# Late attention scores as plain float32 on quarters of the array, three rooms for loads and one store a pair

## The chip, the cores and the metric

The kernel runs on one core of one Trainium2 chip. The metric is the time of one execution on the device, in microseconds (us); less is better. All inputs and the output are float32 in HBM.

## What is computed

Banded attention with a linear bias for 4 batches, 8 heads, 768 positions and 64 numbers a head, and behind it a two-layer perceptron on the 3072 tokens.

```python
scores = (1 / sqrt(D)) * q @ k.T
is_global = pos[None, :] < n_global            # 8
is_local = (rel >= 0) & (rel < n_local)        # 96
dist = where(is_global & ~is_local, n_local, abs(rel))
scores = where(is_global | is_local, scores - slopes[h] * dist, -1e9)
a = exp(scores - max(scores))
x = (a / (sum(a) + 1e-9)) @ v                  # 3072 x 512
h = x @ w_in                                   # 512 x 2048
out = (h * clip(h + 3, 0, 6) / 6) @ w_out      # 2048 x 512
```

## The kernel before

The tokens are cut into 8 blocks of 384 (`TB`), each in three tiles of 128 queries (`NT`). A block has four pairs of heads, so there are 32 pairs, `n` = 0 to 31. A query tile sees 232 keys (`W`): 96 ahead of the tile, 8 global ones, and its own 128. Pairs 0 to 8 (`EARLY`) are early, 9 to 31 late.

The layers. Float32 matrices are split into a high and a low part of type float32r, and a product is three matmuls (high with high, low with high, high with low). For one of 16 slices `f` of the middle dimension, `first` (L168) does 12 matmuls of 384 columns into `hp`; `gate` (ScalarE L179, VectorE L180) makes `g`; `high` makes `gh` (L186 on GpSimd or L188 on ScalarE) and `rest` makes `gl` (L193, VectorE); `second` (L200) does 9 matmuls of 512 columns into `acc`. `twos` takes two slices at a time: both `first` parts, two places for other work ("units"), both `second` parts of the two slices before, two units more. So 32 units make up a block's layers, and the attention of the next block is put into them by `attention`; `rest_of_third` does the same in the stage before, with one slice at a time (a half slice is one unit).

The attention of a pair. `load` brings keys, queries and values into a room (`load0` and so on) in SBUF; keys and queries come first, values when the room's values are used up. Early pairs take their scores as plain float32 on half the rows of TensorE for each head (`scores`, L857). Late pairs split queries and keys first (`split`: L831 ScalarE, L832 GpSimd, L835 and L838 VectorE), both parts one above the other in the rows, and take two float32r matmuls for each head and tile (L861): 12 a pair, 232 columns each (128 for the first tile of a batch). `weigh` adds distances and takes the minimum on VectorE (L872), then the exponential with its sum on ScalarE (L876). `sum_up` (L886, L887, VectorE) inverts the sums, `normalize` (L896, GpSimd) multiplies. Then keys must come into the rows. Early pairs are turned on TensorE (`turn`, L904 and L906, copied out at L908 as `pt`). Late pairs are turned by VectorE in squares of 32 (`spread`, L921), stored to `there` in DRAM (L923, one store a tile), and fetched back in another order (`fetch`, L930, four a pair) as `weights`. `values` (L948) multiplies with v: plain float32, each head on one half of the array's columns, 12 matmuls a pair (10 for the first block of a batch). `put_x` (L154, L155) puts the result into `xh` and `xl`.

In the layers stage, a block's late pairs are six units apart; the values of two pairs stand together behind the second one, six units after its fetch. One bank `sp`, one bank `tp` and one bank `xp` are for attention; a tile's scores for both heads go to one bank, and tiles take `sp` and `tp` in turn.

The early stage is followed by a stage in which the weight matrices are decoded from 64-bit words (`decode`, L410 to L427, mostly VectorE), with layer steps of blocks 0 and 1 in an order written by hand (`ORDER`). Instructions of TensorE, GpSimd and SP keep the order in which the code writes them (`in_order`); those of VectorE and ScalarE are placed by a scheduler.

Of the kernel before, what the change touches and what calls it, by code (L numbers as in the profile page):

```python
# [33 lines left out]
QW = 2 * TB  # L34
# [3 lines left out]
SLOPES = [2.0 ** (-8.0 * (h + 1) / H) for h in range(H)]  # L38
LEAST, MOST = (float(np.uint32(e << 20).view(np.float32)) for e in (896, 1151))
# [4 lines left out]
ROOMS = 2  # L44
# [15 lines left out]
class Kernel:  # L60
# [162 lines left out]
    def attending(self, ctx, heads, rows, ps, **kw):  # L223

        if heads:
            self.hp = self.pool("hp", heads, ctx=ctx, **kw)
# [53 lines left out]

    def rooms(self, pool, n, start=0):

        return [pool.tile([P, LOAD], F32, name=f"load{start + i}") for i in range(n)]
# [4 lines left out]
    def load(self, n, values):  # L288

        if n < len(self.blocks) * NPAIR:  # L290
            end = KW + (TB if n < EARLY else QW)
# [12 lines left out]
    def loaded(self, n):  # L304
# [3 lines left out]
        q = at[:, KW:KW + QW].rearrange("p (j t c) -> p j t c", j=2, t=NT)  # L308
# [30 lines left out]
    def banded_setup(self):  # L339
# [7 lines left out]
        for n in range(ROOMS):  # L347
# [164 lines left out]
    def banded(self, flag):  # L512
# [12 lines left out]
        with ExitStack() as early, ExitStack() as words:  # L525
# [10 lines left out]
            with ExitStack() as ctx:  # L536
                self.room += self.rooms(self.pool("more", 1, ctx=ctx), MORE - ROOMS, ROOMS)
                self.load(2, False)
                self.fetch(1)
                for n in range(ROOMS):  # L540
                    self.load(n, True)
                self.plain_distances(ctx)
                self.attending(ctx, 0, 9, 5)
# [52 lines left out]
            self.weights()  # L596
            self.allowed = 4 * (2 * NF + 1)
# [9 lines left out]
        self.attending(self.ctx, 2, 3, 2, side="right")  # L607
        self.bp = self.pool("bp", 3, side="right")
        self.there = self.pool("there", 2, bass.MemoryType.DRAM)
# [39 lines left out]
    def rest_of_third(self, x, slices):  # L649
# [3 lines left out]
        for k in range(3):  # L653
            pairs[0].split(k, False)
        units[1] += [lambda: self.load_next(EARLY, False)]
        for p, (me, after) in enumerate(zip(pairs, pairs[1:])):
            at = units[4 * p + 1:]
            last = after is pairs[-1]
            at[0] += [lambda t=t, me=me: me.scores(t)() for t in range(NT)]
            at[1] += [me.sum_up] + [lambda t=t, me=me: me.normalize(t) for t in range(NT)]  # L660
            at[2] += [lambda t=t, me=me: me.spread(t) for t in range(NT)] + [me.fetch]
            for k in range(3):
                at[k + 3 if last else k].append(lambda k=k, after=after: after.split(k))
# [4 lines left out]
    def attention(self, i, x, first):  # L668
# [4 lines left out]
        for p in range(NPAIR):  # L673
# [11 lines left out]
            for t in range(1, NT if after else 0):  # L685
                at[t + 3].append(lambda t=t, after=after: after.split(t))
# [115 lines left out]
class Pair:  # L802
# [4 lines left out]
    def __init__(self, kernel, n, x, plain):  # L807
# [4 lines left out]
        self.parts = [{}, {}]  # L812

    def low(self, t):
        return CB if self.tb == 0 and t == 0 else 0

    def split(self, step, load=True):
# [3 lines left out]
        k, q, _, _ = kk.loaded(self.n)  # L821
        c = slice(CB if self.tb == 0 else 0, None)
        for j, part in enumerate(self.parts):
            h = 2 * self.pr + j
            scale = float(-1.0 / (np.sqrt(D) * SLOPES[h]))
            own, other = (slice(0, D), slice(D, P)) if j == 0 else (slice(D, P), slice(0, D))
            if step == 0:
                part["q1"] = kk.hp.tile([P, NT, P], F32R, name="q1")
                part["q2"] = kk.hp.tile([P, NT, P], F32R, name="q2")
                part["kx"] = kk.hp.tile([P, KW], F32R, name="kx")  # L830
                nc.scalar.mul(out=part["q1"], in_=q[:, j], mul=scale)  # L831
                nc.gpsimd.tensor_scalar(out=part["kx"][own, c], in0=k[own, c], scalar1=1.0, scalar2=0.0,  # L832
                                        op0=ALU.mult, op1=ALU.add)
            elif step == 1:
                nc.vector.scalar_tensor_tensor(out=part["q2"], in0=q[:, j], scalar=scale, in1=part["q1"].bitcast(F32),  # L835
                                               op0=ALU.mult, op1=ALU.subtract)
            else:
                nc.vector.tensor_tensor(out=part["kx"][other, c], in0=k[own, c], in1=part["kx"][own, c].bitcast(F32),  # L838
                                        op=ALU.subtract)
        if step == 2 and load:  # L840
            kk.load_next(self.n, False)

    def scores(self, t):
# [3 lines left out]
        if t != 1 or not self.plain:  # L847
            self.banks = [kk.bank("s")[:, 0:2 * W].rearrange("p (i c) -> p i c", i=2) for _ in range(2 if self.plain else 1)]
        sp = [self.banks[j][:, t % 2] if self.plain else self.banks[0][:, j] for j in range(2)]
# [4 lines left out]
        for j in range(2):  # L854
            if self.plain:
                rows = slice(j * D, (j + 1) * D)
                nc.tensor.matmul(sp[j][:, lo:W], lhsT=queries[rows, 0, t], rhs=keys[rows, c], start=True, stop=True)  # L857
            else:
                part = self.parts[j]
                for m, q in enumerate((part["q1"], part["q2"])):  # L860
                    nc.tensor.matmul(sp[j][:, lo:W], lhsT=q[:, t], rhs=part["kx"][:, c], start=(m == 0), stop=(m == 1))  # L861
        return lambda: self.weigh(t, sp, e, lo)

    def weigh(self, t, sp, e, lo):
        nc, kk = self.nc, self.k
        for j in range(2):
# [3 lines left out]
            else:  # L870
                d, scale = (kk.d0 if lo else kk.d1), SLOPES[h]
            nc.vector.tensor_tensor_reduce(out=e[:, j, lo:W], in0=sp[j][:, lo:W], in1=d, op0=ALU.add, op1=ALU.min, scale=scale,  # L872
                                           scalar=3.0e38, accum_out=self.least[:, i:i + 1])
        for j in range(2):
            i = 2 * t + j
            nc.scalar.activation(out=e[:, j, lo:W], in_=e[:, j, lo:W], func=AF.Exp, bias=self.least[:, i:i + 1], scale=-1.0,  # L876
# [12 lines left out]
    def normalize(self, t):  # L889
        nc, e, lo = self.nc, self.rows[t], self.low(t)  # L890
        for j in range(2):
            over = self.sums[:, 1, 2 * t + j:2 * t + j + 1]
            if self.n == 0:
                nc.vector.tensor_scalar(out=e[:, j, lo:W], in0=e[:, j, lo:W], scalar1=over, scalar2=None, op0=ALU.mult)
            else:
                nc.gpsimd.tensor_scalar(out=e[:, j, lo:W], in0=e[:, j, lo:W], scalar1=over, scalar2=0.0, op0=ALU.mult, op1=ALU.add)  # L896
# [14 lines left out]
    def spread(self, t):  # L911
# [3 lines left out]
        if t == 0:  # L915
            self.weights = kk.tp.tile([P, 4, NT, 2, 2, 32], F32, name="weights")
            self.there = kk.there.tile([P, 4, NT, 2, 2 * 32], F32, name="there")
        blocks = kk.bp.tile([P, 4, 2, 2, 32], F32, name="blocks")
        parts = slice(1 if self.low(t) else 0, None)
        for s, c in ((0, 0), (1, CB))[parts]:  # L920
# [107 lines left out]
```

## Time and profile before

| | us |
|---|---|
| median of 3 runs (660.98 to 661.49) | 661.33 |
| the profiled execution | 660.32 |
| its span, first to last instruction | 658.5 |
| TensorE busy (98%) | 647.1 |
| VectorE busy (64%) | 423.2 |
| ScalarE busy (43%) | 286.4 |
| GpSimd busy (29%) | 189.1 |

The stages in that execution: the early pairs to about 59 us, decoding with layers to 151 us, the first three late pairs to 199 us, and layers with the attention of the next block to the end. The granted TensorE clock is 1.000.

How to read the lines below: PE is TensorE, DVE VectorE, ACT ScalarE, POOL GpSimd, SPq the queue of DMA issues on SyncE. L861 is line 861 of the kernel. A piece of the chain gives its start and length in us, engine, tile and line, and how many instructions it merges. A group or a timeline row gives its output and inputs, the part of the array for TensorE (rows by columns), the shape, and, behind the bar, busy us and mean ns, then idle time ahead and what ended it. A matmul's own duration in a row runs to its modelled end; what counts on TensorE is the distance from one start to the next. "xN, KB, us" in the DMA table is the median from issue to landing.

### The profile page before, as it was taken

The page shows a single profiled execution, that of the slowest core. Times are in us where ns is not written, and L with a number is a line of the kernel's source. Part 1 is how long each engine was busy: PE and PEld are TensorE (multiplying, and loading weights), DVE is VectorE, ACT ScalarE, POOL GpSimd, SP SyncE. Part 2 cuts the span into 40 slices and gives each one's busy share as a digit, 9 for nine tenths or more (in the row PEclk, how much of TensorE's full clock was granted, in tenths as well). Part 3 has the DMA queues.
Part 4 walks back from the last instruction along what each step waited for, and adds up shares of the span by engine and source line. Part 5 has one row for each costly group of instructions (what it writes and reads, how often), then busy time and mean ns, then how long its engine had stood idle before and what let it go on. Part 6 is the DMA issues. An engine that isn't in the chain of part 4 may idle for free.

```text
span 658.5 us, 11444 instructions
## 1 busy us (share of the span) xinstructions
PE 647.1 (98%) x3933; PEld 581.0 (88%) x3933; DVE 423.2 (64%) x1147; ACT 286.4 (43%) x752; POOL 189.1 (29%) x377
## 2 busy tenths in 40 slices
PE   9989999999999999999999999999999999999997
PEld 7768899998989999999998999899899999989985
DVE  6888999998766876357654777356763676422222
ACT  6896877776333442244414333143331543121111
POOL 5663000002532433034241444124340342202100
PEclk9999999999999999999999999999999999999999
DMA  8676444432573675427552366615654275400001
GB/s 291 174 233 213 135 157 157 135 125 89 150 222 111 178 188 142 132 88 186 147 156 97 95 178 183 184 52 142 167 137 128 81 185 141 114 31 18 1 1 53
DMA packets 67316, 88.86 MB, mean 135 GB/s; under 512 B 10288, under 2 KB 52016, under 8 KB 67248
## 3 DMA queue, kind: packets, MB, share of 16 engines
q1 hardware_dynamic: 66960, 87.77, 45.9%
q8 instruction: 33, 0.54, 0.3%
q14 instruction: 35, 0.29, 0.1%
q10 hardware_dynamic: 288, 0.26, 0.1%
HBM read 65.08 MB, written 22.94 MB: 134 GB/s over the span
## 4 chain that ended last, share of the span: by engine, by line
PE 85%; DVE 9%; ACT 2%; issue 2%; POOL 1%; DMA 1%; POOLq 0%; DVEq 0%; ACTq 0%
PE hp L168 37%; PE acc L200 33%; PE xp L948 3%; PE sp L861 2%; PE tp L948 2%; PE tp L861 2%; PE sp L200 1%; DVE wz L423 1%; PE tp L200 1%; DVE wz L419 1%; PE xp L200 1%; DVE n L872 1%; ACT n L876 1%; DVE wz L411 1%; DVE g L180 1%
## 5 line engine op out<-in xcount | busy, mean ns | idle before, releaser
L179 ACT ACTIVATE g<-hp,small 128x384 f32<-128x384 f32 x127 | 73.6, 580 | 254.1 <-PE hp L168 147.2
L168 PE MATMUL hp<-xh,w1h 128*128 128x384 f32 x512 | 172.7, 337 | 0.4 <-ACT w1h L427 0.4
L168 PE MATMUL hp<-xh,w1l 128*128 128x384 f32 x512 | 172.3, 337 | 0.5 <-DVE w1l L416 0.5
L168 PE MATMUL hp<-xl,w1h 128*128 128x384 f32 x512 | 171.7, 335 | 0.0
L186 POOL TENSOR_SCALAR gh<-g 128x384 fp32r<-128x384 f32 x104 | 53.3, 512 | 289.1 <-DVE g L180 244.5
L180 DVE SCALAR_TENSOR_TENSOR g<-g,hp 128x384 f32<-128x384 f32 x128 | 70.2, 548 | 99.2 <-ACT g L179 98.8
L200 PE MATMUL acc<-w2h,gl 128*128 128x512 f32 x336 | 132.4, 394 | 0.2 <-DVE gl L193 0.2
L200 PE MATMUL acc<-w2h,gh 128*128 128x512 f32 x336 | 132.6, 395 | 0.0
L200 PE MATMUL acc<-w2l,gh 128*128 128x512 f32 x336 | 131.6, 392 | 0.0
L193 DVE TENSOR_TENSOR gl<-g,gh 128x384 fp32r<-128x384 f32 x128 | 75.9, 593 | 57.4 <-POOL gh L186 47.3
L896 POOL TENSOR_SCALAR n<-n,sums 128x232 f32<-128x232 f32 (+1 forms) x186 | 94.1, 522 | 48.4 <-DVE sums L887 42.5
L876 ACT ACTIVATE n<-n,least 128x232 f32<-128x232 f32 (+1 forms) x192 | 88.6, 464 | 30.4 <-DVE least L872 29.6
L168 PEld LDWEIGHTS hp<-xh,w1h 128*128 128x128 f32 x512 | 96.2, 188 | 3.4 <-ACT w1h L427 0.9
L168 PEld LDWEIGHTS hp<-xl,w1h 128*128 128x128 f32 x512 | 96.2, 188 | 2.1
L168 PEld LDWEIGHTS hp<-xh,w1l 128*128 128x128 f32 x512 | 96.0, 188 | 1.0 <-DVE w1l L416 0.8
L200 PEld LDWEIGHTS acc<-w2h,gl 128*128 128x128 f32 x336 | 63.0, 188 | 15.2 <-DVE gl L193 1.7
L200 PEld LDWEIGHTS acc<-w2h,gh 128*128 128x128 f32 x336 | 63.2, 188 | 13.3 <-issue 1.2
L200 PEld LDWEIGHTS acc<-w2l,gh 128*128 128x128 f32 x336 | 63.2, 188 | 11.6
L921 DVE STREAM_TRANSPOSE blocks<-n 128x256 f32<-128x256 f32 x127 | 49.4, 424 | 25.1 <-POOL n L896 23.1
L832 POOL TENSOR_SCALAR kx<-load 64x504 fp32r<-64x504 f32 (+1 forms) x46 | 29.1, 632 | 117.8 <-PE hp L168 96.1
L876 ACT ACTIVATION_READ_ACCUMULATOR n<-n,least 128x1 f32 x192 | 36.2, 188 | 0.0
L838 DVE TENSOR_TENSOR kx<-load,kx 64x504 fp32r<-64x504 f32 (+1 forms) x46 | 32.9, 715 | 1.8 <-POOL kx L832 0.4
(118 smaller groups left out, 731.5 us busy)
## 6 DMA issues: line engine op xcount, KB each, us to landing
wst<-w SPq DMA_DIRECT2D x32, 512.0 KB, 3.5
there<-blocks SPq DMA_DIRECT2D x58, 256.0 KB, 2.6
load<-pairs SPq DMA_DIRECT2D x23, 636.0 KB, 5.2
load<-pairs SPq DMA_DIRECT2D x32, 384.0 KB, 4.6
weights<-there SPq DMA_DIRECT2D x48, 192.0 KB, 3.6
weights<-there SPq DMA_DIRECT2D x44, 160.0 KB, 3.3
out<-o SPq DMA_DIRECT2D x23, 256.0 KB, 2.1
load<-pairs SPq DMA_DIRECT2D x8, 444.0 KB, 4.7
```

The lines of the kernel that those rows point to most:

```text
L168: self.nc.tensor.matmul(hp, lhsT=self.w1(w, f)[:, kt, :], rhs=a[:, kt, :], start=(n == 0), stop=(n == 3 * NKT - 1))
L179: nc.scalar.activation(out=g, in_=hp, func=AF.Relu, bias=self.three, scale=1.0)
L180: nc.vector.scalar_tensor_tensor(out=g, in0=g, scalar=6.0, in1=hp, op0=ALU.min, op1=ALU.mult)
L186: self.nc.gpsimd.tensor_scalar(out=gh, in0=g, scalar1=1.0, scalar2=0.0, op0=ALU.mult, op1=ALU.add)
L193: self.nc.vector.tensor_tensor(out=gl, in0=g, in1=gh.bitcast(F32), op=ALU.subtract)
L200: self.nc.tensor.matmul(acc[tt], lhsT=a[:, tk], rhs=self.w2(w, f), start=(f == 0 and j == 0), stop=(f == NF - 1 and j == 2))
L832: nc.gpsimd.tensor_scalar(out=part["kx"][own, c], in0=k[own, c], scalar1=1.0, scalar2=0.0, op0=ALU.mult, op1=ALU.add)
L838: nc.vector.tensor_tensor(out=part["kx"][other, c], in0=k[own, c], in1=part["kx"][own, c].bitcast(F32), op=ALU.subtract)
L876: nc.scalar.activation(out=e[:, j, lo:W], in_=e[:, j, lo:W], func=AF.Exp, bias=self.least[:, i:i + 1], scale=-1.0, accum_out=self.sums[:, ...
L896: nc.gpsimd.tensor_scalar(out=e[:, j, lo:W], in0=e[:, j, lo:W], scalar1=over, scalar2=0.0, op0=ALU.mult, op1=ALU.add)
L921: nc.vector.transpose(out=blocks[:, :, s].rearrange("p b j q -> p j b q"), in_=e[:, :, c:c + P].rearrange("p j (b q) -> p j b q", b=4))
L948: nc.tensor.matmul(xps[j * D:(j + 1) * D, t * P:(t + 1) * P], lhsT=vt[0:K, t, j * D:(j + 1) * D], rhs=self.part(t, j, c, K), start=(c == 0 ...
```

## The change

- **Scores of late pairs** (`packed` for `split` and `scores`). Queries are scaled in place on ScalarE (`scale`), by a column of factors `over`. Each tile is cut into four groups of 32 queries, and a group sees 136 keys (96, 8 and 32, `PW`). For each tile, group and head there is one plain float32 matmul, on the 64 rows of its head and the 32 columns of its group: 24 a pair. Head 0 goes to one bank, head 1 to another, all three tiles in each, and all six `weigh` calls follow at once. New masks `dl` for groups are made once on GpSimd (`packed_masks`).
- **Turning.** A group's keys start 32 further for each group, so the turned squares are stored shifted: all three tiles in one store a pair from one `blocks` tile, into two standing tiles `there` whose unused squares are zeroed once (`zeros_ahead`, 12 stores). `fetch` is eight DMAs for four, of half the size.
- **Loads.** Late pairs load their queries once instead of twice, and there are three rooms instead of two, all standing.
- **Places.** The first three late pairs stand three half slices apart instead of four. Sums, normalizing and spreading keep their units in the layers stage.

```diff
-QW = 2 * TB
+QW = TB
+GQ = 32
+GROUPS = P // GQ
+PW = PREV + NG + GQ
-ROOMS = 2
+ROOMS = 3
...
-                 "one": {"s": (o,), "x": (o,)}, "layers": {"s": (s, t), "t": (t,), "x": (x,)}}[self.stage][what]
+                 "one": {"s": (o,), "t": (o,), "x": (o,)}, "layers": {"s": (s,), "t": (t,), "x": (x,)}}[self.stage][what]
...
+    def packed_masks(self):
+        c, ts = self.const, self.nc.gpsimd.tensor_scalar
+        self.dl = c.tile([P, 2, PW], F32, name="dl")
+        self.over = c.tile([P, NPAIR], F32, name="over")
+        for h in range(H):
+            self.nc.gpsimd.memset(self.over[h % 2 * D:(h % 2 + 1) * D, h // 2:h // 2 + 1], float(-1.0 / (np.sqrt(D) * SLOPES[h])))
+        self.nc.gpsimd.memset(self.dl[:, 0], FAR)
...
+    def zeros_ahead(self):
...
+        nc.gpsimd.memset(zeros, 0.0)
...
@@ rest_of_third
-        for k in range(3):
-            pairs[0].split(k, False)
+        pairs[0].scale()
...
-            at = units[4 * p + 1:]
+            at = units[3 * p + 1:]
-            at[0] += [lambda t=t, me=me: me.scores(t)() for t in range(NT)]
+            at[0] += [me.packed, lambda me=me: self.load_next(me.n, False)]
@@ attention
-            for t in range(NT):
-                at[t].append(lambda t=t, me=me: me.scores(t)())
-            if after:
-                at[3].append(lambda after=after: after.split(0))
+            at[0] += [me.packed, lambda me=me: self.load_next(me.n, False)]
...
-            for t in range(1, NT if after else 0):
-                at[t + 3].append(lambda t=t, after=after: after.split(t))
+            if after:
+                at[4].append(after.scale)
...
+    def scale(self):
+        _, q, _, _ = kk.loaded(self.n)
+        nc.scalar.mul(out=q, in_=q, mul=kk.over[:, self.pr:self.pr + 1])
+
+    def packed(self):
+        banks = [kk.bank(b)[:, 0:NT * PW].rearrange("p (t c) -> p t c", t=NT) for b in "st"]
+        keys, queries, _, _ = kk.loaded(self.n)
+        for t in range(NT):
+            for g in range(GROUPS):
+                own, c = slice(g * GQ, (g + 1) * GQ), t * TG + g * GQ
+                for j in range(2):
+                    rows = slice(j * D, (j + 1) * D)
+                    nc.tensor.matmul(banks[j][own, t], lhsT=queries[rows, t, own], rhs=keys[rows, c:c + PW], start=True, stop=True,
+                                     tile_position=(j * D, g * GQ))
+        for t in range(NT):
+            self.weigh(t, [bank[:, t] for bank in banks], kk.up.tile([P, 2, PW], F32, name="n"), 0)
...
@@ spread, when t is the last tile
+            nc.sync.dma_start(out=bass.AP(tensor=there.tensor, offset=there.offset,
+                                          ap=[[GQ * row + SHIFT * step, GROUPS], [row, GQ], [1, 4 * step]]),
+                              in_=self.blocks.rearrange("p b s t j q -> p (b s t j q)"))
@@ fetch
+        for s in range(2):
+            for b in range(4):
+                rows = NG if s == 1 and b == 3 else 32
+                nc.sync.dma_start(out=to[32 * b:32 * b + rows, :, s],
+                                  in_=there[:, b + (0 if s else AHEAD), s].rearrange("(a p) c -> p a c", a=4)[0:rows])
```

The changed lines move down in the file: L857 becomes L882, L861 becomes `packed`'s L864, L908 becomes L929, L948 becomes L974.

TensorE, the first late pair, in the order before (the last layer matmul ahead, the 12 matmuls, the first one behind):

```order
L200 MATMUL acc<-w2h_1028,gl 128x512
L861 MATMUL acc<-kx,q_1963 128x128
L861 MATMUL acc<-kx,q_1964 128x128
L861 MATMUL acc<-kx,q_1968 128x128
L861 MATMUL acc<-kx,q_1969 128x128
L861 MATMUL acc<-kx,q_1963 128x232
L861 MATMUL acc<-kx,q_1964 128x232
```

and in the changed kernel at the same place:

```order
L206 MATMUL acc<-w2h_1026,gl 128x512
L864 MATMUL acc<-load_72 32x136 x24
L174 MATMUL hp<-xh,w1h_1024 128x384
L174 MATMUL hp<-xl,w1h_1024 128x384
L174 MATMUL hp<-xh,w1l_1025 128x384
```

Twelve matmuls (the six that follow are of 232 columns as well) have become 24 of 32 by 136, in one row since only their places differ; layer matmuls stand right ahead and behind in both.

ScalarE near the end of the early stage, before (L908 copies the turned tiles `pt`, L376 and L427 decode, L188 is the `gh` cast):

```order
L427 CAST w1h_143<-wz 128x4x128
L376 ACTIVATE wz<-wst 128x512
L188 CAST gh<-g 128x384
L908 COPY pt<-tp 128x512
L376 ACTIVATE wz<-wst 128x512
```

and in the changed kernel (L410, L461, L194, L929 are the same four lines):

```order
L410 ACTIVATE wz<-wst 128x512
L461 CAST w1h_144<-wz 128x4x128
L194 CAST gh<-g 128x384
L850 ACTIVATE load_72<-load_72,over 128x384
L850 ACTIVATE load_73<-load_73,over 128x384
L850 ACTIVATE load_74<-load_74,over 128x384
L929 COPY pt<-tp 128x512
L410 ACTIVATE wz<-wst 128x512
```

The scalings of the first three late pairs stand between the `gh` cast and the copy of `pt`.

SP in the layers stage, one pair and its neighbours, before:

```order
L293 DMA load_72<-pairs 128x1272
L923 DMA there<-blocks 512x1x128 x3
L930 DMA weights<-there 32x4x384 x4
L293 DMA load_73<-pairs 128x1272
L293 DMA load_73<-pairs 128x768
```

and in the changed kernel:

```order
L327 DMA load_74<-pairs 128x888
L944 DMA there_1975<-blocks 4x32x1536
L956 DMA weights<-there_1975 32x4x192 x7
L956 DMA weights<-there_1975 8x4x192
L327 DMA load_73<-pairs 128x768
```

One store stands for three, and eight fetches for four; the loads stay around them.

More of the change, by code (lines that the diff above doesn't have):

```diff
@@ L279, in banded_masks @@
         nc.gpsimd.tensor_copy(out=d1[:, PREV:CB], in_=glo)
+    def packed_masks(self):
[6 more added lines that the diff above has]
+        for g in range(GROUPS):
+            rows, start = slice(g * GQ, (g + 1) * GQ), g * GQ
+            for out, d in ((self.dl[rows, 0, CB - start:], self.d0[rows, 0:start + GQ]),
+                           (self.dl[rows, 1], self.d1[rows, start:start + PW])):
+                ts(out=out, in0=d, scalar1=1.0, scalar2=0.0, op0=ALU.mult, op1=ALU.add)
+    def zeros_ahead(self):
+        nc, pool = self.nc, self.pool("there", 1, bass.MemoryType.DRAM)
+        self.there = [pool.tile([P, SPREAD, 2, NT * 64], F32, name=f"there{i}") for i in range(2)]
+        zeros = self.bp.tile([P, 4, 2, NT, 2, 32], F32, name="blocks")[:, 0:AHEAD, 0].rearrange("p b t j q -> p b (t j q)")
+        nc.gpsimd.memset(zeros, 0.0)
+        for there in self.there:
+            for g in range(GROUPS):
+                own, k = slice(g * GQ, (g + 1) * GQ), g * SHIFT
+                if k > 0:
+                    nc.sync.dma_start(out=there[own, 0:k, 1], in_=zeros[own, 0:k])
+                if k < AHEAD:
+                    nc.sync.dma_start(out=there[own, k + 4:, 0], in_=zeros[own, k:])
     def rooms(self, pool, n, start=0):
@@ L346, in banded_setup @@
         nc.scalar.dma_start(out=self.iv, in_=self.bounds.broadcast_to([P, 4]))
-        for n in range(ROOMS):
+        for n in range(2):
             self.load(n, False)
@@ L606, in banded @@
             self.decoded_to(2 * NF - 1)
-        self.attending(self.ctx, 2, 3, 2, side="right")
-        self.bp = self.pool("bp", 3, side="right")
-        self.there = self.pool("there", 2, bass.MemoryType.DRAM)
+        self.attending(self.ctx, 3, 2, side="right")
+        self.bp = self.pool("bp", 1, side="right")
+        self.zeros_ahead()
         self.op = self.pool("op", 3, side="right")
@@ L811, in __init__, with first @@
         self.sums, self.rows, self.pts = None, [], []
-        self.parts = [{}, {}]
+        self.end = W if plain else PW
+    def first(self, t):
+        return self.tb == 0 and t == 0
     def low(self, t):
-        return CB if self.tb == 0 and t == 0 else 0
-    def split(self, step, load=True):
+        return CB if self.plain and self.first(t) else 0
+    def scale(self):
         nc, kk = self.nc, self.k
[L821 to L841, printed above, removed]
@@ L846, in scores @@
             self.sums = kk.up.tile([P, 2, 2 * NT], F32, name="sums")
-        if t != 1 or not self.plain:
-            self.banks = [kk.bank("s")[:, 0:2 * W].rearrange("p (i c) -> p i c", i=2) for _ in range(2 if self.plain else 1)]
-        sp = [self.banks[j][:, t % 2] if self.plain else self.banks[0][:, j] for j in range(2)]
+        if t != 1:
+            self.banks = [kk.bank("s")[:, 0:2 * W].rearrange("p (i c) -> p i c", i=2) for _ in range(2)]
+        sp = [self.banks[j][:, t % 2] for j in range(2)]
         e = kk.up.tile([P, 2, W], F32, name="n")
@@ L854, in scores @@
         for j in range(2):
[L855 to L861, printed above, removed]
+            rows = slice(j * D, (j + 1) * D)
+            nc.tensor.matmul(sp[j][:, lo:W], lhsT=queries[rows, t], rhs=keys[rows, c], start=True, stop=True)
         return lambda: self.weigh(t, sp, e, lo)
     def weigh(self, t, sp, e, lo):
-        nc, kk = self.nc, self.k
+        nc, kk, end = self.nc, self.k, self.end
         for j in range(2):
@@ L875, in weigh @@
             i = 2 * t + j
-            nc.scalar.activation(out=e[:, j, lo:W], in_=e[:, j, lo:W], func=AF.Exp, bias=self.least[:, i:i + 1], scale=-1.0,
+            nc.scalar.activation(out=e[:, j, lo:end], in_=e[:, j, lo:end], func=AF.Exp, bias=self.least[:, i:i + 1], scale=-1.0,
                                  accum_out=self.sums[:, 0, i:i + 1])
@@ L889, in normalize @@
     def normalize(self, t):
-        nc, e, lo = self.nc, self.rows[t], self.low(t)
+        nc, e, lo, end = self.nc, self.rows[t], self.low(t), self.end
         for j in range(2):
@@ L936, in part @@
             return self.pts[t][0:K, j, c, :]
-        return self.weights[0:K, :, t, 1 - c, j]
+        return self.weights[0:K, :, c, t, j]
     def values(self, bank="x"):
@@ L943, in values @@
         for t in range(NT):
-            two = not self.low(t)
+            two = not self.first(t)
             for c in range(2 if two else 1):
```

60 lines of the change are left out of this document (28 added, 32 removed).

## The prediction

> **What bounds the kernel now.** I read the page first: its busy line, then the chain that ended last.
>
> ```profile
> PE 647.1 (98%) x3933; PEld 581.0 (88%) x3933; DVE 423.2 (64%) x1147; ACT 286.4 (43%) x752; POOL 189.1 (29%) x377
> ...
> PE 85%; DVE 9%; ACT 2%; issue 2%; POOL 1%; DMA 1%; POOLq 0%; DVEq 0%; ACTq 0%
> ```
>
> TensorE carries the end, so the change is worth what it does to TensorE's own time, plus any wait it gives TensorE. Next comes the chain in order of time, in one stretch of the late stage (start, us, what):
>
> ```profile
> 209.44 4.13 PE acc L200 x18
> 213.57 0.44 PE tp L861 x4
> 214.02 0.45 PE sp L861 x4
> ...
> 218.63 0.44 PE tp L861 x4
> ...
> 237.05 1.47 PE xp L948 x24
> 238.53 1.32 PE tp L948 x24
> 239.84 4.33 PE acc L200 x18
> ```
>
> Every piece is TensorE, one behind the other: layer pieces of 4.1 us, the scores of a pair in three pieces (L861) and the values of two pairs (L948). The source view of the scores gives their number:
>
> ```profile
> L861 PE MATMUL sp<-kx,q x140: 222/274/373, 203.1 to 558.9; 128*128 128x232 f32 x116, 128*128 128x128 f32 x24
> ...
> L861 PE MATMUL tp<-kx,q x100: 223/273/323, 203.6 to 554.3; 128*128 128x232 f32 x92, 128*128 128x128 f32 x8
> ...
> L861 PE MATMUL acc<-kx,q x36: 222/274/337, 159.2 to 179.9; 128*128 128x232 f32 x24, 128*128 128x128 f32 x12
> ```
>
> 140 + 100 + 36 = 276 matmuls, 12 for each of 23 late pairs. A pair costs 0.44 + 0.45 + 0.44 = 1.33 us of TensorE in the open: 30.6 us in all.
>
> **Term 1: the scores on TensorE.** A pair now has 24 plain float32 matmuls of 136 columns, each on 64 rows and 32 columns of the array, eight different places before a place comes again. The trace has no such form, so I build it from three rows. Plain float32 on half the rows stands in the early pairs (counts from the source view, then a piece of TensorE's timeline):
>
> ```profile
> L857 PE MATMUL acc<-load x72: 272/356/591, 5.1 to 40.9; 64*128 64x232 f32 x62, 64*128 64x128 f32 x10
> ...
> L857 PE MATMUL sp<-load x36: 272/356/591, 5.1 to 40.5; 64*128 64x232 f32 x26, 64*128 64x128 f32 x10
> ```
>
> ```profile
> 40.31 0.36 PE L857 MATMUL sp<-load 64*128 64x232 f32 x1
> 40.32 0.36 PE L857 MATMUL acc<-load 64*128 64x232 f32 x1
> 40.51 0.36 PE L857 MATMUL sp<-load 64*128 64x232 f32 x1
> 40.52 0.75 PE L857 MATMUL acc<-load 64*128 64x232 f32 x5
> ```
>
> Nine early pairs of six matmuls are 54, and there are 108 records: a plain float32 matmul is two passes. A pass of 232 columns takes 0.20 us (40.31 to 40.51), or 0.86 ns a column, and two matmuls on different rows run side by side, started 0.01 us apart. Different columns of the array run side by side too: the values above are 12 matmuls of 128 columns, 24 passes, in 1.32 us, where one pass of 128 columns takes 0.11 us alone (chain, transposes of the early pairs):
>
> ```profile
> 45.66 0.11 PE hp L906
> 45.77 0.11 PE hp L904
> ```
>
> 24 x 0.11 would be 2.6 us; they take half of that. So rows in two and columns in two are each shown without loss; rows in two times columns in four are not.
>
> A new pass is 136 x 0.86 = 0.117 us. With eight places at once a pair is 48 / 8 = 6 passes deep: 0.70 us, and 0.05 us for starting the other places 0.01 us apart. Going from the whole array to parts of it and back has a price: the first L948 piece takes 1.47 us and the second 1.32, and the L200 piece behind takes 4.33 where 4.13 is usual. That is 0.15 + 0.20 = 0.35 us an excursion, and each late pair gets a new one, since its scores stand between layer pieces. [...]
>
> A pair: 0.70 + 0.05 + 0.35 = 1.10 us for 1.33, so 0.23 us less, times 23 = **-5.3 us**. [...] I take eight, since each of the two ways of sharing runs without loss.
>
> **Term 2: a wait that goes.** The first late pair of the layers stage asks for a score bank a second time too early (TensorE's timeline):
>
> ```profile
> 203.56 0.60 PE L861 MATMUL tp<-kx,q 128*128 128x232 f32 x4
> 204.54 0.71 PE L861 MATMUL sp<-kx,q 128*128 128x232 f32 x4 [0.38 <-DVE least L872]
> ```
>
> Four of these take 0.44, so 0.54 us are lost. Now a pair takes its two banks once: **-0.5 us** (between 0 and -0.5).
>
> **Term 3: the scaling on ScalarE.** The splits of a pair (two of L831, and L832, L835, L838) become one in-place scaling. By the order, those of the first three late pairs stand together on ScalarE, in the middle of the early stage, behind the second gh cast before the copy `pt`. There the chain runs over ScalarE:
>
> ```profile
> 57.69 0.41 ACT gh L188
> 58.09 0.49 ACT pt L908
> 58.58 0.14 issue
> 58.72 0.30 PE tp L904
> ```
>
> ```profile
> L831 ACT ACTIVATE q<-load 128x384 fp32r<-128x384 f32 x46 | 21.5, 517 | 25.2 <-issue 9.2 <-PE sp L861 6.4 <-PE acc L861 5.1
> ...
> 64.42 0.67 ACT L376 ACTIVATE wz<-wst 128x512 f32<-128x512 f32 x1 [2.04 <-DMA wst<-w]
> ```
>
> Three of 0.517 put up to 1.5 us ahead of `pt`, and TensorE waits for it at 58.72. They also wait for `over`, which GpSimd writes behind its last decode step. ScalarE itself makes it good at 62 us, where it idles 2.04 us for a load; TensorE can make it good only where it later waits for the decoding (DVE's 9% of the chain). Between 0 and 1.5: **+0.7 us**.
>
> **What costs nothing.** The removed work was beside TensorE:
>
> ```profile
> L832 POOL TENSOR_SCALAR kx<-load 64x504 fp32r<-64x504 f32 (+1 forms) x46 | 29.1, 632 | 117.8 <-PE hp L168 96.1
> L876 ACT ACTIVATION_READ_ACCUMULATOR n<-n,least 128x1 f32 x192 | 36.2, 188 | 0.0
> L838 DVE TENSOR_TENSOR kx<-load,kx 64x504 fp32r<-64x504 f32 (+1 forms) x46 | 32.9, 715 | 1.8 <-POOL kx L832 0.4
> ```
>
> GpSimd idles 96.1 us ahead of its first kx: the new masks and the zeroed tile go in there. Weighing, exponentials and normalizing get shorter with 136 columns for 232. In the order the sums now stand right behind the six weighings on VectorE, so VectorE waits there for six exponentials; queued behind are `g` and `gl` of the next layer pieces, which TensorE wants only after a further 4.13 us piece: covered. The twelve zero stores go out while no late pair is ready. Loads shrink and go one room earlier.
>
> **The sum.** -5.3 - 0.5 + 0.7 = -5.1 us on the span of 658.5, so 653.4; the profiled execution, 1.8 us longer than its span, would read 655.2. The median of before is 661.33, 1.0 above its profiled execution; the same step gives **656.2**.
>
> **Rivals.**
>
> *Fewer places at once* (slower). TensorE keeps four of eight places going: 12 x 0.117 + 0.02 + 0.35 = 1.77 us a pair, +0.44 x 23 = +10.1, with the other terms 671.6. It decides when fewer than 48 x 0.117 / (1.33 - 0.35) = 5.7 places run on average. For it: more than two at once is never seen. Against it: two at once loses nothing, in rows or in columns. Chance 0.17.
>
> *Starts too close together* (slower). The 48 passes want a start every 0.015 us. Rows show 0.01 us between two neighbours (40.31, 40.32), and, held up as long, 0.055 us (1.32 / 24), which the passes explain alone. Break-even is 0.98 / 48 = 0.020 us; the middle of the two rows, 0.032, gives 1.56 + 0.35 = 1.91 us a pair, +13.3, and 674.8. Chance 0.05. [...]
>
> *Weights back too late* (slower, or the gain gone). The store of a pair is now one of 768 KB behind the last transpose, and eight fetches follow for four; SP and GpSimd before, around the last pair of a block, and the DMA table:
>
> ```profile
> 410.88 2.26 SPq L923 DMA_DIRECT2D there<-blocks  x3
> 415.40 1.74 SPq L930 DMA_DIRECT2D weights<-there  x4
> ```
>
> ```profile
> 407.24 1.31 POOL L832 TENSOR_SCALAR kx<-load 64x400 fp32r<-64x400 f32 x2
> 408.65 3.14 POOL L896 TENSOR_SCALAR n<-n,sums 128x232 f32<-128x232 f32 x6
> ```
>
> ```profile
> load<-pairs SPq DMA_DIRECT2D x23, 636.0 KB, 5.2
> ...
> weights<-there SPq DMA_DIRECT2D x48, 192.0 KB, 3.6
> ```
>
> ```profile
> 421.05 1.47 PE xp L948 x24
> 422.52 1.32 PE tp L948 x24
> ```
>
> Now the last fetch is issued at about 416.7 and lands 3.6 later, at 420.3; its reader starts at 422.52: 2.2 us to spare. Four more issues of 0.43 cost 1.7; one store of 768 KB, between the 5.2 us of a 636 KB load and 5.2 x 768 / 636 = 6.3, some 5.7 us, against 2.8 from the last third's issue (412.6) to 415.40, costs 2.9; the reader comes 0.44 earlier. That is 5.0. Gained: the kx ahead of the normalizing on GpSimd, the splits on VectorE, and a third tile that is weighed a layer piece earlier, an estimated 3.3 us from where `gh` of that piece can be done. Left: 0.5 us. If half of the 3.3 comes, TensorE waits some 1.2 us at the second values of five blocks and hardly at the first: +6.0, 662.2; if none of it, 2.8 us five times and less at the first values, past 670. Behind the waiting fetch on SP stand only loads and output stores with whole blocks to spare. Chance 0.13.
>
> *More than forecast.* [...] Chance 0.07.
>
> **The numbers.** The forecast has 0.58; with 0.95 to 1.25 us a pair its own range is 651.5 to 660. It and the better case hold 0.65; up to 669 come most of the late weights and the edge of the two packing rivals: about 0.8 in 650 to 669. A change under 0.2% (1.3 us) can't be told from none here; the three runs before lie 0.5 us apart. Faster: the forecast, the better case and the mildest late weights, 0.66. Same: 0.07. Slower: both packing rivals and the rest of the late weights, 0.27.
>
> **What would show it.** Right: in the chain after, the 24 matmuls of a pair take about 1.1 us together with the longer piece behind them; eight start within 0.1 us in the timeline; no wait of the values' first matmul for a DMA; a gap of about 1 us near 58 us that wasn't there. Wrong: 12 steps of 0.117 in a pair (four places), even spacing above 0.02 us without overlap (starts), or waits for `weights` ahead of the values (late weights).

## The result, and the profile after

| | before | after |
|---|---|---|
| median, us | 661.41 (660.98 to 661.69) | 811.56 (810.2 to 814.81, 4 runs) |
| the profiled execution, us | 660.32 | 810.2 |
| its span, us | 658.5 | 808.4 |
| TensorE idle in it, us | 11.4 | 116.8 |
| granted TensorE clock (share of full speed) | 1.000 | 0.919 |

The ratio is 1.2278 (95% interval 1.2237 to 1.2319): 150 us slower, where 5 us faster was forecast. The page of after, its busy line, the clock in 40 slices and the chain by engine and line:

```profile
PE 691.6 (86%) x4761; PEld 599.8 (74%) x4761; DVE 354.8 (44%) x1066; ACT 266.4 (33%) x729; POOL 153.6 (19%) x349
...
PEclk9999999998899878998888979889997899899999
...
DMA 37%; PE 36%; DVE 8%; SPq 8%; POOL 4%; ACT 4%; issue 3%; POOLq 0%; ACTq 0%; DVEq 0%
```

Before, 85% of the chain was TensorE; now transfers hold the largest share. TensorE's idle time grew by 105.4 us (span less busy, in both pages) and its busy time by 44.5, with less work in it: that is the clock. The chain in order of time, in one stretch of the late stage (start, us, what):

```profile
343.20 11.29 DMA there<-blocks
...
358.62 11.84 DMA there<-blocks
...
374.16 3.45 DMA load<-pairs
377.74 0.48 issue
378.21 0.56 ACT g L185
...
405.60 11.29 DMA there<-blocks
...
420.10 2.14 DMA weights<-there
422.37 1.55 PE sp L974 x12
```

One store of a pair takes 11.3 us to land, where the prediction had some 5.7. After two stores the chain runs over a load into ScalarE's `g`, after another over the fetched weights into the values. The queue of SP in the same stretch shows how load and fetch come behind the store:

```profile
343.20 0.53 SPq L944 DMA_DIRECT2D there<-blocks  x1
354.51 3.56 SPq L956 DMA_DIRECT2D weights<-there  x8
358.17 0.36 SPq L327 DMA_DIRECT2D load<-pairs  x1
358.62 0.52 SPq L944 DMA_DIRECT2D there<-blocks  x1
```

SP stands from 343.73 to 354.51 at the first fetch, which waits for the store; then come eight issues, and only then the load. ScalarE's timeline (line, operation, count, and in brackets idle time ahead and what ended it):

```profile
362.47 0.61 ACT L850 ACTIVATE load<-load,over 128x384 f32<-128x384 f32 x1 [12.64 <-DMA load<-pairs]
362.99 0.56 ACT L185 ACTIVATE g<-hp,small 128x384 f32<-128x384 f32 x1
```

The scaling of a later pair's queries waits 12.64 us for its load, and the gate `g`, which TensorE needs now, is queued behind it. The waits of after, in total, times and longest, put the two side by side:

```profile
ACT load L850 <- DMA load<-pairs: 145.6, 16, 13.8
...
PE sp L974 <- DMA weights<-there: 52.2, 20, 5.7
...
PE hp L174 <- DVE g L186: 37.4, 10, 7.2
...
DVE blocks L939 <- DMA there<-blocks: 36.6, 9, 8.3
```

What a store does on the 16 DMA engines is in the DMA view: 40 slices, tenths of the 16 engines that are busy. The first two lines are after's, from the issue of one store to the fetch (343.2 to 354.6):

```profile
DMA  0020320321213221213221222222232313111100
...
DMA packets 133, 0.80 MB, mean 70 GB/s; under 512 B 4, under 2 KB 4, under 8 KB 132
```

and these are before's, for the three stores of a pair (409 to 416):

```profile
DMA  0000000000000000039999999999999992000000
...
DMA packets 1585, 0.79 MB, mean 112 GB/s; under 512 B 49, under 2 KB 1585, under 8 KB 1585
```

Before, the same 0.79 MB keeps the engines busy for some 3 us (17 slices of 0.175). After, about a quarter of them are busy for some 10 us: four of the store's 128 packets of 6 KB are under way for 7.6 of the 9.8 us from the first to the last, and never more than five. The outermost count of the store is four, its groups.

### The profile page after: what moved, and what is told of

The parts are those of the page before. It is cut to its first block, busy times and chain, and to the rows that moved or that the text cites. A ratio compares the mean times of both kernels' runs of the same rounds, so it can differ in the third digit from the quotient of the medians.

```text
span 808.4 us, 12987 instructions
## 1 busy us (share of the span) xinstructions
PE 691.6 (86%) x4761; PEld 599.8 (74%) x4761; DVE 354.8 (44%) x1066; ACT 266.4 (33%) x729; POOL 153.6 (19%) x349
## 4 chain that ended last, share of the span: by engine, by line
DMA 37%; PE 36%; DVE 8%; SPq 8%; POOL 4%; ACT 4%; issue 3%; POOLq 0%; ACTq 0%; DVEq 0%
DMA there<-blocks 31%; PE hp L174 15%; PE acc L206 15%; SPq L956 7%; DMA load<-pairs 4%; DVE blocks L939 3%; POOL n L917 3%; ACT n L897 2%; DMA weights<-there 2%; PE sp L974 1%; ACT g L185 1%; POOL gh L192 1%; DVE g L186 1%; PE sp L206 1%; PE tp L206 1%
## 5 line engine op out<-in xcount | busy, mean ns | idle before, releaser
L174 PE MATMUL hp<-xh,w1h 128*128 128x384 f32 x512 | 181.0, 353 | 37.4 <-DVE g L186 37.4
L174 PE MATMUL hp<-xh,w1l 128*128 128x384 f32 x512 | 177.7, 347 | 0.1
L174 PE MATMUL hp<-xl,w1h 128*128 128x384 f32 x512 | 177.3, 346 | 0.0
L206 PE MATMUL acc<-w2h,gh 128*128 128x512 f32 x336 | 140.8, 419 | 0.0
L206 PE MATMUL acc<-w2l,gh 128*128 128x512 f32 x336 | 137.8, 410 | 0.0
L897 ACT ACTIVATE n<-n,least 128x136 f32<-128x136 f32 (+2 forms) x192 | 79.5, 415 | 75.3 <-DVE least L893 74.6
L917 POOL TENSOR_SCALAR n<-n,sums 128x136 f32<-128x136 f32 (+2 forms) x186 | 81.4, 454 | 44.8 <-DVE sums L908 23.7
L974 PE MATMUL sp<-weights,load 128*64 128x128 f32 (+1 forms) x224 | 28.4, 419 | 52.2 <-DMA weights<-there 52.2
L974 PEld LDWEIGHTS sp<-weights,load 128*64 128x64 f32 (+1 forms) x224 | 21.4, 215 | 57.6 <-issue 56.1
L850 ACT ACTIVATE load<-load,over 128x384 f32<-128x384 f32 x23 | 13.9, 614 | 146.2 <-DMA load<-pairs 145.6
```

The costliest lines, as they stand in the source:

```text
L174: self.nc.tensor.matmul(hp, lhsT=self.w1(w, f)[:, kt, :], rhs=a[:, kt, :], start=(n == 0), stop=(n == 3 * NKT - 1))
L206: self.nc.tensor.matmul(acc[tt], lhsT=a[:, tk], rhs=self.w2(w, f), start=(f == 0 and j == 0), stop=(f == NF - 1 and j == 2))
L850: nc.scalar.mul(out=q, in_=q, mul=kk.over[:, self.pr:self.pr + 1])
L897: nc.scalar.activation(out=e[:, j, lo:end], in_=e[:, j, lo:end], func=AF.Exp, bias=self.least[:, i:i + 1], scale=-1.0, accum_out=self.sums ...
L917: nc.gpsimd.tensor_scalar(out=e[:, j, lo:end], in0=e[:, j, lo:end], scalar1=over, scalar2=0.0, op0=ALU.mult, op1=ALU.add)
L974: nc.tensor.matmul(xps[j * D:(j + 1) * D, t * P:(t + 1) * P], lhsT=vt[0:K, t, j * D:(j + 1) * D], rhs=self.part(t, j, c, K), start=(c == 0 ...
```

## The experiments

In the diffs, `-` is the changed kernel and `+` the experiment, unless another kernel is named. e1 to e4 ran beside a median of before of 661.03, e5 to e8 of 660.61, e9 and e10 of 661.01, e11 of 661.12; ratios are to these.

**e1, four stores a pair.**

```diff
-            nc.sync.dma_start(out=bass.AP(..., ap=[[GQ * row + SHIFT * step, GROUPS], [row, GQ], [1, 4 * step]]), in_=self.blocks...)
+            for g in range(GROUPS):
+                nc.sync.dma_start(out=bass.AP(..., offset=there.offset + g * (GQ * row + SHIFT * step),
+                                              ap=[[row, GQ], [1, 4 * step]]), in_=self.blocks[g * GQ:(g + 1) * GQ]...)
```

> The changed kernel with the pair's store written as four stores, one for each group of 32 rows; rows (6144 bytes), bytes and squares are the same. Theory A (shape): a store is spread over DMA engines by its outermost dimension; four groups outermost keep four engines busy, 32 rows outermost keep 16. Then the stores land in 3 to 5 us instead of 11.3, no DMA piece of the store of over 5 us stands in the chain, and the kernel takes 654 to 664 us, as the terms of the prediction on TensorE would have it. Theory B (size): 768 KB in rows of 6 KB take 11 us however they are written. Then nothing changes: over 790 us.

Measured: 671.96 (670.56 to 678.59), ratio 1.0165 (1.0138 to 1.0192), span 676.8 in the profiled execution. So 140 of the 150 us went with the store's shape (the same bytes go to the same places, as four stores); but the kernel is still slower than before, above the range given. The DMA view of one pair's four stores, of 32 rows outermost each (250.5 to 255.4, 40 slices):

```profile
DMA  0000000990799059909990098995989163000000
...
DMA packets 192, 0.79 MB, mean 161 GB/s; under 512 B 64, under 2 KB 64, under 8 KB 192
```

In 14 slices 9 tenths or more of the 16 engines are busy, where after has 2 or 3 tenths in 24 of 40; and the longest piece of a store in the chain is 4.92 us, where after has pieces of 11.3. What is left is on ScalarE. Its source view for the scaling, and TensorE's for the scores (x, ns min/median/max, first and last start):

```profile
L850 ACT ACTIVATE load<-load,over x23: 599/616/618, 58.5 to 533.4; 128x384 f32<-128x384 f32 x23
...
  DMA load<-pairs: 78.2, 17
```

```profile
L864 PE MATMUL sp<-load x480: 276/276/316, 209.1 to 572.6; 64*32 64x136 f32 x160
```

The last scaling starts at 533.4, its scores 39 us later, at 572. The scheduler puts the scaling about where the load is issued, far ahead of the need, and so ScalarE waits for transfers in which nobody is yet interested: 78.2 us in 17 waits.

**e2, the store cut in two half rows, with four groups outermost as before.**

```diff
+            for half in range(2):
+                nc.sync.dma_start(out=bass.AP(..., offset=there.offset + half * 2 * step,
+                                              ap=[[GQ * row + SHIFT * step, GROUPS], [row, GQ], [1, 2 * step]]),
+                                  in_=self.blocks[:, half * 2:half * 2 + 2]...)
```

> The changed kernel with the store cut into two of half the row (3072 bytes), each still with the four groups outermost. Theory A: both halves stay on four engines, the second lands no earlier than the one store did, and the kernel stays within 3% of 811 us. Theory B: each is half the size in rows of half the length, the two run side by side, a landing of 6 to 7 us, and the kernel comes to 700 to 740 us.

Measured: 835.21 (833.57 to 836.85), ratio 1.2628 (1.2596 to 1.2661), 2.9% above the changed kernel. Two stores in place of one help nothing as long as each has four outermost.

**e3, one store with 128 rows outermost, without the shift.**

```diff
+            nc.sync.dma_start(out=bass.AP(..., ap=[[row, P], [1, 4 * step]]), in_=self.blocks...)
```

> The changed kernel with one store a pair of the same bytes and rows of 6144 bytes, but with 128 rows outermost, since the squares of all groups go to the same place of their row (the shift by group is left out, so the weights that come back are others; every unused square is zeroed ahead). Theory A: lands in 4 to 6 us, the kernel takes 654 to 668 us. Theory B: one store of the same size and rows, so 11 us and about 811 us.

Measured: 660.17 (658.81 to 662.43), ratio 0.999 (0.9977 to 1.0003). This kernel leaves the shift out, so its weights are others; its time still counts for the store. The same bytes from the same rows in one store: the size of the store is not what is slow. e1, e2 and e3 together single out the outermost count. With four outermost a store takes 11.3 us (after); here, with 128, the longest piece of one in the chain is 5.58 us.

**e4, e1 with the scaling held.** The scaling gets an order behind the last gate on ScalarE ahead of it in the code, which is the only edit against e1.

```diff
         nc.scalar.mul(out=q, in_=q, mul=kk.over[:, self.pr:self.pr + 1])
+        kk.tc.add_manual_dep(nc.cur_bb.bb.instructions[-1], kk.last_gate, ... NoSync ...)
```

> As e1, and the scaling of a pair's queries is held behind the last gate on ScalarE, so that the first three no longer stand in the early stage. If those three cost TensorE their 1.5 us near 58 us and nothing gives it back, 1.0 to 1.5 us less than e1; if the later waits for decoding give it back, within 0.4 us of e1. Theory B changes nothing here: over 790 us, as e1.

Measured: 654.96 (654.26 to 655.97), ratio 0.9908 (0.989 to 0.9926). That is 17 us less than e1, over ten times what was expected, and faster than the kernel before. The expectation had only priced the three scalings of the early stage; the gain came from the others, as e6 and e7 show. Where they stand now:

```profile
L851 ACT ACTIVATE load<-load,over x23: 602/607/609, 152.6 to 541.5; 128x384 f32<-128x384 f32 x23
```

```profile
L867 PE MATMUL sp<-load x480: 276/276/302, 203.1 to 548.2; 64*32 64x136 f32 x160
```

The last scaling is 6 us ahead of its scores (the first pair of a block still some 25), and no wait of a scaling for a load is left in the list of waits.

**e5, e4's held scaling with the changed kernel's own slow store.**

> The changed kernel with its own single store of four groups, but every scaling held behind the last gate on ScalarE, as in e4. Theory A: two separate losses were added up, the slow store making the weights late, and the scaling that stands on ScalarE far ahead of its need and waits for loads that SP issues late. With the scaling held only the first loss is left. In e4 the second pair of each two has 10.2 to 11.4 us from the start of its store to its values; with a store that lands 11.3 us after its issue of 0.5, eight fetch issues of 0.43 and a landing of 2.1 it needs 17.4, so 6 to 7 us are missing ten times, and some 12 in the three first pairs: 655 + 66 + 12 = 733 (715 to 755). Waits for weights ahead of the values stay in the list of waits, waits of the scaling for loads are gone. Theory B, the store alone makes the whole loss and the scaling adds only what it added in e1 (17 us): 811.6 - 17 = 795. Theory C, the late loads on ScalarE make the whole loss: under 665.

Measured: 765.2 (763.44 to 767.95), ratio 1.1581 (1.1547 to 1.1615). Between theories A (733) and B (795). TensorE is idle for 87.9 us (764.1 less 676.2 busy) for 13.9 in e4, 74 more where 78 were expected. So the waits were sized rightly in sum; one by one they are not the 6 to 7 us expected ten times, but by turns 7 to 10 and 4 to 5 us. The list of waits (total us, times, longest):

```profile
PE sp L977 <- DMA weights<-there: 62.5, 20, 9.4
```

What was left out is TensorE's clock after a wait. One of them in TensorE's timeline, the layer piece behind it in the chain, and the windows around it (window, its us, TensorE busy and its instructions, granted clock, DMA share, GB/s):

```profile
360.94 1.12 PE L977 MATMUL sp<-weights,load 128*64 128x128 f32 x8 [7.76 <-DMA weights<-there]
```

```profile
364.25 6.45 PE acc L207 x18
```

```profile
348.00:361.00 13.00, 5.24 (x45) 0.77 0.32 105
361.00:362.60 1.60, 1.05 (x8) 0.50 0.88 167
362.60:368.50 5.90, 5.80 (x22) 0.50 0.62 217
368.50:376.00 7.50, 7.50 (x82) 0.98 0.23 87
```

For nearly 8 us from the end of the wait the clock is 0.50. The `acc` piece takes 6.45 us where 4.13 is usual. The busy lines of e5 and of e4:

```profile
PE 676.2 (88%) x4761; PEld 588.9 (77%) x4761; DVE 354.9 (46%) x1066; ACT 268.4 (35%) x729; POOL 153.1 (20%) x349
```

```profile
PE 638.6 (98%) x4761; PEld 563.7 (86%) x4761; DVE 357.0 (55%) x1066; ACT 268.7 (41%) x729; POOL 154.1 (24%) x349
```

That is 37.6 us more for the same instructions. Here the clock is 0.50 behind a wait of 7.76 us. A shorter wait can stand ahead of it too: in after the clock is 0.50 from 60.0 to 63.3 us, behind a wait of 2.35 us, while one of 2.41 us, which ends at 364.19, leaves it at 1.00.

**e6 and e7, e1 with the scaling held for the first three late pairs alone, and for the others alone.**

```diff
+        if self.n < EARLY + 3:      # e6;  e7: if self.n >= EARLY + 3:
+            kk.tc.add_manual_dep(...)
```

> e1 (four stores) with only the scaling of pairs 9 to 11 held behind the last gate, those of pairs 12 to 31 left where the scheduler puts them. Theory A, the gain of e4 over e1 (17 us) comes from pairs 12 to 31, whose scaling stands on ScalarE 35 to 63 us ahead of its scores in e1's trace and waits for loads just issued: this run keeps nearly all of the loss, 669 to 672; it gains only what term 3 of the prediction gave for the three in the early stage, 0 to 1.5 us. Theory B, the three in the early stage are the whole of it, since a delay near 58 us shifts the decoding and all behind it: 655 to 658.

> The other half of e4: e1 with the scaling of pairs 12 to 31 held, those of pairs 9 to 11 left in the early stage near 58 us. Theory A: 655 to 657, that is e4's time plus the price of three scalings of 0.6 us ahead of the copy on which TensorE waits near 58 us, by term 3 of the prediction +0.7 (0 to 1.5). Theory B: 668 to 672.

Measured: e6 671.71 (670.9 to 673.87), ratio 1.0176 (1.0155 to 1.0197); e7 655.39 (654.75 to 656.83), ratio 0.9925 (0.9909 to 0.9942). Theory A in both: the loss is with the pairs from 12 on. e7 also shows term 3 by itself. The chain near 58 us, in e7:

```profile
57.86 1.62 ACT load L851 x3
59.48 0.47 ACT pt L933
...
60.09 0.30 PE tp L929
```

and in e4, which has no scaling there:

```profile
58.03 0.49 ACT pt L932
...
58.66 0.30 PE tp L928
```

TensorE comes 1.43 us later in e7. Compared start by start, 0.6 us of it are left at 150 us, behind the last waits for decoding, and nothing at 198 us, where TensorE waits for the third late pair's weights in both. The spans, 653.0 and 652.5, differ by less than those of e4's own executions (652.5 to 654.2).

**e8, e4 with the matmuls of head 0 first, then those of head 1.**

```diff
-        for t in range(NT):
-            for g in range(GROUPS):
-                for j in range(2):
+        for j in range(2):
+            for t in range(NT):
+                for g in range(GROUPS):
```

> e4 with the 24 packed matmuls of a pair in another order: all twelve of head 0 (rows 0 to 63), then all twelve of head 1, so that a place of the array comes again after four matmuls instead of eight. Nothing else differs. Theory A, eight places run side by side and a pair is as deep as the passes of its fullest place: 12 passes instead of 6, 6 x 0.117 = 0.70 us more a pair, 16.1 us in 23 pairs, 671 (669 to 673), and in the timeline of TensorE each pair shows twelve steps of 0.117 us. Rival, the array keeps two matmuls of one place apart by less than a whole pass, or what counts is the number of starts: 655 to 657.

Measured: 658.56 (658.24 to 659.38), ratio 0.9967 (0.9955 to 0.998): 3.6 us more than e4, not 16. Neither side had it. TensorE's timeline of one pair (`sp` is head 0, `tp` head 1; a row's count is of passes, 24 for each head):

```profile
211.80 0.55 PE L867 MATMUL sp<-load 64*32 64x136 f32 x12
212.09 0.32 PE L867 MATMUL tp<-load 64*32 64x136 f32 x4
212.18 0.30 PE L867 MATMUL sp<-load 64*32 64x136 f32 x4
...
212.46 0.53 PE L867 MATMUL tp<-load 64*32 64x136 f32 x12
212.91 0.44 PE L174 MATMUL hp<-xh,w1h 128*128 128x384 f32 x1
```

In the program all of head 0 stands ahead of head 1. But head 1 starts at 212.09, when only 12 of head 0's 24 passes have started, and then both run side by side. So a pair is some eight steps deep instead of six, not twelve: the first scores to the next layer matmul take 1.11 us (211.80 to 212.91) for 0.89 in e4, which is two steps of 0.12 us more.

**e9, e4 with one store of 128 rows, the shift in the fetches.** Each row of `there` keeps zeros on both sides, and a fetch reads each group one square earlier than the group ahead of it.

```diff
+            nc.sync.dma_start(out=there[:, AHEAD:AHEAD + 4].rearrange("p b s c -> p (b s c)"), in_=self.blocks...)
...
+                nc.sync.dma_start(out=to[32 * b:32 * b + rows, :, s],
+                                  in_=bass.AP(..., offset=at, ap=[[row, rows], [GQ * row - SHIFT * step, GROUPS], [1, step // 2]]))
```

> e4 with the store as the change means it, one a pair, but all 128 rows outermost as in e3; the shift of a group's squares by 32 keys is put into the fetches, which read each group one place earlier (the zeros ahead and behind are stored by 4 instead of 12). The full result is computed. Theory A, only the outermost count of the store was wrong: one such store is issued in 0.33 to 0.37 us and lands as fast as e3's, so nothing of the weights is late, and with the held scaling the time is that of e4 or a little less: three issues of 0.41 a pair fall away, 12 us before the values that nothing waits for in the layers, and of the 1.1 us that TensorE waits for weights in e4 at the first late pairs a part may go: 654 to 655.2. Rival, the fetches become slow, since their reads now run over rows of different groups at different places: their median landing of 2 us grows, waits for weights come back, over 657.

Measured: 652.81 (652.69 to 653.08), ratio 0.9877 (0.986 to 0.9893), the fastest of all, and a little below the range given. The DMA view of one store (213.7 to 217.2, 40 slices):

```profile
DMA  0000200009919989899599599896995000000000
...
DMA packets 145, 0.79 MB, mean 227 GB/s; under 512 B 16, under 2 KB 16, under 8 KB 144
```

The same large packets are done in some 1.9 us (22 slices of 0.0875), and in 14 of these slices 9 tenths or more of the engines are busy. Compared start by start on TensorE, e9 is 1.1 us ahead of e4 from the third late pair's values on. Of this 0.3 us come from a layer matmul at 187 us and 0.8 from the wait for weights there, which is 0.33 us in e9 and in e4

```profile
197.89 0.88 PE L978 MATMUL acc<-weights,load 104*64 104x128 f32 x12 [1.09 <-DMA weights<-there]
```

The other 1 us between the medians isn't explained by the two profiles, whose spans are 1.4 us apart.

**e10, e5 with two `blocks` tiles.**

```diff
-        self.bp = self.pool("bp", 1, side="right")
+        self.bp = self.pool("bp", 2, side="right")
```

> e5 with two tiles blocks instead of one. e5 took 765 where 733 was expected; its list of waits shows VectorE waiting 68.9 us for stores before it may write blocks again. Theory A, that wait is the missing part: it holds up the distances, g and gl that stand behind it on VectorE. With two tiles it goes, and the weights that come 6 to 7 us late ten times stay: 728 to 745. Theory B, SP is the bound, which a pair now keeps for 16 us of waiting and issuing, and VectorE's wait only shows it: the time stays within 2% of 765.

Measured: 764.98 (764.29 to 767.25), ratio 1.157 (1.155 to 1.1589), the same as e5: theory A falls. TensorE's busy time stays at 674.5 and its idle time at 91.0 (765.5 less 674.5). VectorE's wait for the store is gone from the list of waits, and nothing is gained: it only lay beside the wait for weights. What e5 had over its forecast is the clock, above. That SP is the bound, as theory B says, isn't shown by this.

**e11, the changed kernel with only its store mended, as in e9.**

> The changed kernel with nothing else mended than its store, in the way of e9 (128 rows outermost, the shift in the fetches); the scaling stays where the scheduler puts it. It is the fourth corner of a square: the changed kernel 811.6, the scaling held alone 765 (e5), both 652.8 (e9). Theory A, with a store that lands in some 3 us the loads are issued early enough that ScalarE's waits for them are short, but the scaling still stands 38 us and more ahead of its scores: as e3, 659 to 661, so the store is nearly the whole of the 150 us and the scaling the last 7. Rival, e3 read its squares in another order than the full kernel and was slower or faster for that: under 656 or over 664.

Measured: 659.42 (657.52 to 662.76), ratio 0.9972 (0.9954 to 0.9989). With it the square is closed:

| median, us | scaling left to the scheduler | scaling held |
|---|---|---|
| store with 4 outermost | 811.6 (after) | 765.2 (e5) |
| store with 128 outermost | 659.4 (e11) | 652.8 (e9) |

The two losses feed each other: holding the scaling is worth 46 us beside the slow store, since each load waits for it on SP, and 6.6 beside the fast one. Between them lie the four stores of e1 and e4, with 17 us. Why e1 is 12.5 us slower than e11, when its stores with their four issues keep SP only some 1.5 us longer a pair (4.8 for 3.3), was not followed up.

## Why the prediction was wrong, and what in it was right

**The step that failed** is in the rival of late weights: "one store of 768 KB, between the 5.2 us of a 636 KB load and 5.2 x 768 / 636 = 6.3, some 5.7 us". It landed in 11.3. The price was scaled by bytes from a load that has 128 rows outermost; the store has four. The diff showed this, `[GQ * row + SHIFT * step, GROUPS]` stands first in its pattern, and nothing was asked of it. The spare time then was not "0.5 us" left but some 5 short, and the rival that had 0.13 and stopped at "past 670" was what happened: late weights alone take the kernel to 765.2 (e5). e1, e2, e3 and e9 show that it is the outermost count, and not the bytes, the places they go to or the number of stores.

**A second step failed** in the same paragraph: "Behind the waiting fetch on SP stand only loads and output stores with whole blocks to spare". The loads have that time by their scores. But the scaling reads them first, and the scheduler had put it right where the load is issued; ScalarE then waits in order, with `g` behind it (12.64 us for one load in after). The order had shown this for the first three late pairs, as term 3 says, and the prediction didn't ask the same of the other twenty. e4, e6 and e7 show it: 17 us in e1.

**A third cost was not thought of.** A wait of TensorE was priced at its length. The traces add a time at a granted clock of 0.50 with the long ones (with every wait of 4 us or more in after, and behind the one of 7.76 us in e5): 37.6 us of busy time in e5 and, since the instructions are the same, 691.6 - 638.6 = 53 us in after.

**The forecast's own sum held**, once both losses are out of the way. It put the span at 653.4 and the time at 656.2; e7, which has the three terms and neither loss, has 653.0 and 655.39. That it comes so close is in part luck, as the terms show. Term 1 in e4's timeline of TensorE, one pair between layer pieces:

```profile
212.15 0.39 PE L207 MATMUL acc<-w2h,gl 128*128 128x512 f32 x1
212.47 0.30 PE L867 MATMUL sp<-load 64*32 64x136 f32 x1
...
212.51 0.30 PE L867 MATMUL tp<-load 64*32 64x136 f32 x1
212.60 0.28 PE L867 MATMUL sp<-load 64*32 64x136 f32 x1
...
213.15 0.28 PE L867 MATMUL tp<-load 64*32 64x136 f32 x1
213.36 0.45 PE L174 MATMUL hp<-xh,w1h 128*128 128x384 f32 x1
213.64 0.34 PE L174 MATMUL hp<-xl,w1h 128*128 128x384 f32 x1
```

Eight starts lie within 0.04 us (212.47 to 212.51), and the next eight follow 0.13 us behind: eight places side by side, as forecast. The last layer matmul would have been followed at 212.38 (0.23 after its start); the next one starts at 213.36, and the one behind it 0.28 later instead of 0.17. That is 0.98 + 0.11 = 1.09 us a pair, where the prediction had 1.10 (it was 1.33). Within it two small errors cancel: the passes take 0.80 us (212.47 to 213.15, and 0.12 for the last) for 0.75, and going to parts of the array and back 0.29 for 0.35. Both packing rivals are refuted by this. A cheaper pair, on which the better case rests, is shown by no run: e4 has these 1.09 us. Taken so over all 23 pairs, the scores cost 31.7 us in the trace of before and 25.3 in e4's: 6.4 less, for 5.3 + 0.5 of terms 1 and 2 together. Term 2's wait is gone: the first pair of the layers stage takes 0.99 us, like the others. Term 3 was +0.7; it is 0.6 at 150 us and nothing behind 198 us (e7). What stands there instead is a wait that the sum did not have, for the third late pair's weights: 0.85 us in e7 and 1.09 in e4. What was said to cost nothing on GpSimd and VectorE shows no new wait of TensorE in e4.

## What to carry to other kernels

Price a DMA by the outermost dimension of its pattern before its bytes: fold a shift or a group into the side that keeps 128 rows outermost (here the same 768 KB took 3.3 us for 11.3). When work is moved to an engine whose order a scheduler sets, look where each new instruction stands against the transfer that it waits for, and hold it near its need. Price a long wait of TensorE above its length, for the clock behind it (in e5 0.50 for nearly 8 us, behind a wait of 7.76).

## What the runs showed that was not expected

A single DMA of 768 KB takes 11.3 us from its issue with four outermost (after, 70 GB/s on average) and, where nothing else moves, 3.3 us with 128 outermost (e9, 227 GB/s over the 3.5 us of the view), in packets of the same size.

In e8's trace TensorE starts plain float32 matmuls of different places out of the program's order: head 1's first start 0.29 us behind head 0's, with 12 passes of head 0 still to start. Steps on one place stay about 0.12 us apart in both orders.

Beside the slow store, holding an instruction of 0.6 us on an engine that is 33% busy was worth 46 us: its cost was in what stood behind it.
